# Feeding the first two token blocks of a fused layer partly from SBUF, squares taken from the sum, and the last gate moved to the activation

## The chip, the cores and the metric

The kernel runs on one core of a Trainium2 chip. Its engines are TensorE (PE in the profile; its weight loads are PEld), VectorE (DVE), ScalarE (ACT), GpSimd (POOL) and SyncE (SP), whose queue issues nearly all DMA transfers here. The metric is the device time of one execution in microseconds (us), as the median of several runs. A profile shows one execution; its span runs from the first to the last recorded instruction.

## What is computed

The reference is one layer with adaptive layer norm (batch 1, 2048 tokens, 448 channels, all float32):

```python
mod = (_silu(c) @ w_mod).reshape(c.shape[0], 6, 1, -1)
sa, ca, ga, sb, cb, gb = (mod[:, 0], mod[:, 1], mod[:, 2], mod[:, 3], mod[:, 4], mod[:, 5])
h = _layernorm(x, axis=-1) * (1 + ca) + sa
x = x + ga * _A_ref(h, ...)      # S4D convolution along the tokens, by FFT
h = _layernorm(x, axis=-1) * (1 + cb) + sb
x = x + gb * _B_ref(h, B_w1, B_b1, B_w2, B_b2)
```

`_A_ref` builds a kernel of length 2048 for each channel, convolves `h` with it by transforms of length 4096 and adds a skip term. `_B_ref` normalizes `h` once more, multiplies it along the token axis by `w1` (2048 to 1792), adds `b1`, applies the tanh form of GELU, multiplies by `w2` (1792 to 2048) and adds `b2`. The gate `gb`, one value for each channel, is `mod[5]` in the kernel.

## The kernel before

**Stages.** The first half of the time builds the convolution kernels and the spectrum of the input. Then comes the stage of the *pieces*. Piece n handles two of 32 frequency groups for one half of the channels (`DC` = 224 of 448): pieces 0 to 15 are the first half and run mixed with the stage before, pieces 16 to 31 the second half and run in the loop `for k in range(NP + 1)`. For each piece, `pc_load` fetches its spectrum `u` (3 buffers) and its tables `si` (4 buffers), `pc_tables` makes the missing table quarters on POOL, `pc_swap` makes a swapped copy of `u` on ACT, `pc_s2` transforms the kernel's part (`kx`, two PE products), `pc_mul` multiplies on DVE (`z`), `pc_inv` transforms back (`vv`, four PE products of 128x224), and `pc_out` copies the result from PSUM to a tile `vt` on ACT and writes it to `v_d` in HBM. `v_d` has 32 rows (frequency groups) of 128 by 448. In step k of the loop the kernel loads piece n + 3 (n = 16 + k), does `pc_s2` and `pc_mul` of n, the tables of n + 1, and `pc_inv` and `pc_out` of n - 1.

**Norm stage.** The last transform runs along the 32 frequency groups, so each of the 16 token blocks of 128 needs all 32 rows of `v_d`. For block r, `ln_load(r)` reads a tile `vt` of 128 partitions (32 groups by 4) and 2 times 448 columns back from `v_d`, and for odd r the next pair of `x` tiles (`x_pair`). `ln_y(r)` multiplies it by the table `ft` into PSUM (`y`, one buffer, two halves of 64 rows) and adds it to `x` on DVE with the sum taken along. `stats` then makes the mean (DVE), the sum of squares (ACT, `Square` with the mean as bias) and the root. `ln_mod(r)` applies the first norm and the modulation and takes the second statistics; `ln_out(r)` makes `h3`, split into a rounded part `h3h` and a rest `h3l`, so that each product becomes three products in the fast float format. `warm(n)` issues n dummy products.

**First product.** `mlp1` multiplies step r by seven tiles `acc` of PSUM, three products each, 21 in all. Weights come through `WeightStream`: load (SP), rounding (ACT), rest (DVE), four steps ahead. There are two halves of 16 steps with seven tiles each. Behind each, `gelu` reads the tiles: ACT makes `u` (3 buffers), DVE casts it to `uh` and subtracts for `ul`. PE goes on with the next half, whose tiles are the same PSUM banks.

**Second product.** For each of 16 token tiles, 42 products run into `o`; DVE then adds `b2`, multiplies by `mod[5]` and adds `x` read back from HBM, and the result is written out.

**Order.** PE, ACT, DVE and POOL execute in the order of the program text. SP's order is made by a scheduler up to the last four steps of the piece loop and written by hand from there, in two manual regions (`last` and `first`); a transfer without a dependence can still be lifted ahead of the second region. An instruction that waits holds up all behind it on its engine.

The lines that the prediction follows are L828 (`v_d<-vt`, the write of a piece), L1230 (the load of a block), L1250 (`y`), L1253 (adding `x`), L1240 and L1242 (mean and squares), L1222 to L1224 (`acc`), L1294 (`warm`), L1336 to L1338 (`gelu`), L1368 and L1369 (the end).

Of the kernel before, what the change touches and what calls it, by code (L numbers as in the profile page):

```python
# [22 lines left out]
P = 128  # L23
# [8 lines left out]
DC = 224  # L32
# [5 lines left out]
WAHEAD = 4  # L38


def dft_tables():
# [66 lines left out]
    order = lambda a: a.reshape(P, 32, 2, 2, 2, 16).swapaxes(3, 4)  # L108
# [11 lines left out]
    t["FT"] = ft.reshape(P, 64)  # L120

# [99 lines left out]
def tile_adaln_s4d_mixer(ctx, tc, i, out):  # L221
# [20 lines left out]
    with ExitStack() as es:  # L242
# [580 lines left out]
        def pc_out(n, copy=S.copy):  # L823
            c, p = divmod(n, NP)
            vt = swp.tile([P, 2, DC], F32, tag="vt", name="vt", bufs=4) if c else fp.tile([P, 2, DC], F32, tag="vt", name="vt")
            copy(vt, pv.pop(n))
            rows = v_d[2 * p : 2 * p + 2, :, c * DC : (c + 1) * DC]
# [342 lines left out]
        swp = es.enter_context(tc.tile_pool(name="swp", bufs=2))  # L1170
        pc_swap(NP)
        for k in range(NP + 1):
# [16 lines left out]

            if k == NP - 3:  # L1190
                wst.load()
                x_pair(0)

# [9 lines left out]
    with ExitStack() as es:  # L1203
# [9 lines left out]
        v_v = v_d.rearrange("k (ch g r) d -> r (k ch) g d", ch=4, g=2)  # L1213
# [12 lines left out]
        vts, hs, sa, sb = {}, {}, {}, {}  # L1226

        def ln_load(r):
            vts[r] = rot.tile([P, 2, D], F32, tag="vt", name="vt", bufs=4)
            nc.sync.dma_start(vts[r], v_v[r])  # L1230
            if r % 2 and 1 < r < 15:
                x_pair(r + 1)
# [4 lines left out]
        def stats(src, total, tag):  # L1237

            mean, ss, rs = (small(nm, tag) for nm in ("mean", "ss", "rs"))
            V.tensor_scalar(mean, total, -1.0 / D, None, ALU.mult)  # L1240
            sq = rot.tile([P, D], F32, tag="sq", name="sq")
            S.activation(sq, src, AF.Square, bias=mean, accum_out=ss)  # L1242
            S.activation(rs, ss, AF.Sqrt, scale=1.0 / D, bias=eps_t)
            return mean, rs

        def ln_y(r):
            y = py.tile([P, D], F32, tag="y", name="y")
            vt = vts.pop(r)
            for g in range(2):
                nc.tensor.matmul(y[64 * g : 64 * g + 64], ft, vt[:, g], start=True, stop=True)  # L1250
# [33 lines left out]
        for r in range(4):  # L1284
            ln_load(r)
            if r == 1:
                x_pair(2)
# [8 lines left out]
        for t in range(-3, 16):  # L1296
            if t < 0:
                warm((9, 1, 2)[t + 3])
# [33 lines left out]
        def gelu(acc, fh):  # L1332
            for f in range(7):
                k = 7 * fh + f
                u = ru.tile([P, D], F32, tag="u", name="u")
                S.activation(u, acc[f], AF.Gelu_apprx_tanh, bias=b1[:, k : k + 1])  # L1336
                V.tensor_copy(uh[fh][:, f], u)
                V.tensor_tensor(ul[fh][:, f], u, uh[fh][:, f].bitcast(F32), ALU.subtract)  # L1338
# [14 lines left out]
        for t in range(16):  # L1353
# [14 lines left out]
            V.scalar_tensor_tensor(y, o, b2[:, t : t + 1], mod[5], ALU.add, ALU.mult)  # L1368
# [29 lines left out]
```

## Time and profile before

| | |
|---|---|
| median of 3 runs | 698.07 us (697.39 to 699.43) |
| profiled execution | 699.5 us, its span 697.7 us |
| mean granted TensorE clock | 0.988 |
| PE busy | 646.5 us (93%) |
| DVE, ACT, POOL busy | 424.1, 448.5, 274.7 us |
| DMA moved | 128.04 MB, mean 184 GB/s |

A row of the timeline reads: start in us, duration in us, engine, line, operation, output<-inputs, the shape, how often, and in brackets how long the engine stood idle before it and what released it. Rows that follow each other closely are merged (x2, x4), and their duration is then that of the group; a float32 product shows as two records, so x2 is one such product. A row of the chain reads: start, duration, what. In the table by stretches a row has the stretch, its length, the busy time of PE, PEld, DVE, ACT and POOL with the count of instructions, the granted clock, the mean busy share of the 16 DMA engines, and GB/s. A group row has the line, engine, operation, count, busy us and mean ns of one, then the idle time before them.

### The profile page before, as it was taken

The numbers are of one execution on the slowest core, as the hardware profiler recorded it, in microseconds if no ns is written. First come the engines' busy times: TensorE is split into PE (matmuls) and PEld (weight loads), VectorE is DVE, ScalarE is ACT, GpSimd is POOL, SyncE is SP. The second block draws the span as 40 slices with busy tenths as digits, with TensorE's granted clock in tenths as the row PEclk, the third lists the DMA queues.
The fourth block names the chain that finished last, engine by engine and source line by source line (L and its number), as shares of the span: only waits on it lengthen the run. The fifth ranks groups of instructions, "written<-read, shape, count | busy, mean of one in ns | idle before, by whom it ended". The sixth has DMA issues, their size and how long they took to land.

```text
span 697.7 us, 18532 instructions
## 1 busy us (share of the span) xinstructions
PE 646.5 (93%) x7314; PEld 486.1 (70%) x7314; DVE 424.1 (61%) x811; ACT 448.5 (64%) x841; POOL 274.7 (39%) x364
## 2 busy tenths in 40 slices
PE   0868999999988899999999989999999999999997
PEld 0444454455545676676789747778999999999996
DVE  7877889787575584857744368777622354444431
ACT  5787698899879899999766568877422332222220
POOL 6694669588588767777546200000000000000000
PEclk9998999999999999999999999999999999999999
DMA  7595647588785486554579899974683445555640
GB/s 183 178 194 143 214 163 241 212 234 268 213 266 165 126 170 170 145 157 120 142 235 301 257 278 244 236 177 135 174 247 108 146 132 159 159 158 165 169 129 28
DMA packets 101894, 128.04 MB, mean 184 GB/s; under 512 B 13547, under 2 KB 85231, under 8 KB 101807
## 3 DMA queue, kind: packets, MB, share of 16 engines
q1 hardware_dynamic: 100606, 123.31, 63.0%
q0 software_dynamic: 1200, 3.54, 2.4%
q8 instruction: 58, 0.95, 0.6%
q14 instruction: 30, 0.24, 0.1%
HBM read 91.46 MB, written 34.87 MB: 181 GB/s over the span
## 4 chain that ended last, share of the span: by engine, by line
PE 68%; ACT 10%; DMA 8%; DVE 6%; issue 4%; POOL 3%; SPq 1%; DVEq 0%; ACTq 0%; POOLq 0%
PE xe L621 7%; PE acc L1222 7%; PE o L1365 6%; PE o L1364 6%; PE o L1366 6%; PE acc L1223 6%; PE acc L1224 6%; PE kg L711 6%; DMA si<-in_SK_dram 3%; PE xg L621 3%; PE pu L542 2%; PE pu L574 2%; PE vv L820 2%; PE kx L804 2%; PE vv L821 2%
## 5 line engine op out<-in xcount | busy, mean ns | idle before, releaser
L206 ACT CAST whi<-w 128x896 fp32r<-128x896 f32 x64 | 59.8, 938 | 134.9 <-PE o L1365 84.6
L215 DVE TENSOR_TENSOR wlo<-w,whi 128x896 fp32r<-128x896 f32 x64 | 68.1, 1088 | 43.1 <-ACT whi L206 36.8
L684 POOL TENSOR_TENSOR G<-mag,gs 128x512 f32<-128x512 f32 x56 | 71.9, 1283 | 50.9 <-ACT gs L680 47.1
L1222 PE MATMUL acc<-h3h,whi 128*128 128x448 f32 x224 | 82.7, 369 | 0.8 <-ACT h3h L1273 0.8
L1223 PE MATMUL acc<-h3l,whi 128*128 128x448 f32 x224 | 81.5, 364 | 0.7 <-DVE h3l L1280 0.5
L1365 PE MATMUL o<-ul,whi 128*128 128x448 f32 x224 | 81.3, 363 | 0.0
L1364 PE MATMUL o<-uh,whi 128*128 128x448 f32 x224 | 81.2, 362 | 0.0
L1224 PE MATMUL acc<-h3h,wlo 128*128 128x448 f32 x224 | 80.7, 360 | 0.0
L1366 PE MATMUL o<-uh,wlo 128*128 128x448 f32 x224 | 80.6, 360 | 0.0
L711 PEld LDWEIGHTS kg<-E,G 128*32 128x32 f32 x3584 | 56.6, 114 | 32.3 <-issue 22.2
L711 PE MATMUL kg<-E,G 128*32 128x64 f32 x3584 | 66.4, 228 | 6.7 <-issue 6.1
L685 POOL TENSOR_TENSOR G<-mag,gs 128x512 f32<-128x512 f32 x56 | 71.8, 1282 | 0.0
L621 PE MATMUL xg<-tab,lph 64*128 64x512 f32 x112 | 62.3, 556 | 5.1 <-ACT gs L680 2.4
L621 PE MATMUL xe<-tab,lph 64*128 64x512 f32 x112 | 62.2, 555 | 1.1 <-ACT gs L681 0.9
L686 DVE TENSOR_TENSOR E<-m,xe 128x512 f32<-128x512 f32 x53 | 36.4, 687 | 41.3 <-ACT xe L679 24.3
L1368 DVE SCALAR_TENSOR_TENSOR y<-o,b,mod 128x448 f32<-128x448 f32 x16 | 10.9, 684 | 80.2 <-PE o L1366 80.2
L665 POOL TENSOR_TENSOR m<-mag,w 128x512 f32<-128x512 f32 x53 | 56.0, 1056 | 4.3 <-DMA u<-us_d 0.2
L1222 PEld LDWEIGHTS acc<-h3h,whi 128*128 128x128 f32 x224 | 42.0, 188 | 13.9 <-ACT h L1278 5.6
L812 DVE TENSOR_TENSOR z<-kx,u 128x448 f32<-128x448 f32 x48 | 28.4, 620 | 27.7 <-PE kx L804 27.7
L1223 PEld LDWEIGHTS acc<-h3l,whi 128*128 128x128 f32 x224 | 42.1, 188 | 3.3 <-DVE h3l L1280 0.8
L1364 PEld LDWEIGHTS o<-uh,whi 128*128 128x128 f32 x224 | 42.0, 188 | 3.4
L621 PE MATMUL xe<-tab,lex 64*128 64x512 f32 x56 | 28.9, 531 | 16.6 <-DMA lex<-wm 15.8
(233 smaller groups left out, 1512.1 us busy)
## 6 DMA issues: line engine op xcount, KB each, us to landing
w<-in_B_w_dram SPq DMA_DIRECT2D x64, 224.0 KB
w<-in_B_w_dram SPq DMA_DIRECT2D x32, 448.0 KB
u<-us_d SPq DMA_DIRECT2D x48, 224.0 KB
yu_d<-yt SPq DMA_DIRECT2D x16, 448.0 KB
yi<-yu_d SPq DMA_DIRECT2D x32, 224.0 KB
us_d<-uo SPq DMA_DIRECT2D x16, 448.0 KB
v_d<-vt SPq DMA_DIRECT2D x32, 224.0 KB
vt<-v_d SPq DMA_DIRECT2D x16, 448.0 KB
```

Source lines behind the costliest of these rows:

```text
L206: self.nc.scalar.copy(hi, w)
L215: eng.tensor_tensor(lo, w, hi.bitcast(F32), ALU.subtract)
L621: T.matmul(out[k], lhs[r], rhs[r], start=start, stop=stop)
L684: G.tensor_tensor(Gt[:, 1], mg_, v32(sg), ALU.mult)
L685: G.tensor_tensor(Gt[:, 0], mg_, v32(cg_), ALU.mult)
L711: T.matmul(kg[32 * q : 32 * q + 32, m], Gt[:, c, d], E[:, c, d], start=h == 0 and c == 0 and m == 0, stop=h == 1 and c == 1, skip_group_ch ...
L1222: nc.tensor.matmul(acc[f], hi[:, fs], h3h[:, r], start=r == 0, stop=False)
L1223: nc.tensor.matmul(acc[f], hi[:, fs], h3l[:, r], start=False, stop=False)
L1224: nc.tensor.matmul(acc[f], lo[:, fs], h3h[:, r], start=False, stop=r == 15)
L1364: nc.tensor.matmul(o, hi[:, ks], uh[kh][:, k], start=kh == 0 and k == 0, stop=False)
L1365: nc.tensor.matmul(o, hi[:, ks], ul[kh][:, k], start=False, stop=False)
L1366: nc.tensor.matmul(o, lo[:, ks], uh[kh][:, k], start=False, stop=kh == 1 and k == 6)
```

## The change

1. **Blocks 0 and 1 don't wait for the last three pieces.** For these two blocks only 26 of the 32 rows of `v_d` are read for the second half of the channels (`v_load(r, 26)`, issued in step `NP - 2`); the last six rows of the first half of the channels come by four small loads in step 1. The missing products for the last three pieces are taken from their tiles `vt`, still in SBUF (`vlast`), times tables `fl` (masked so that each piece's rows meet only those of the block): six products of 128x128 by 224 columns for each block. `fl` is zeroed on POOL in three parts, and a quarter is loaded, in step 1.
2. **The rows of a token block lie together.** The order of the tables `I1` and `I2` is changed so that a block's 8 rows in each frequency group are contiguous in `v_d`; a load has 128 rows of 3584 bytes where it had 256 of 1792.
3. **Order.** The region `first` begins with `x_pair(2)` and then loads blocks 2 and 3. The nine dummy products before the first `y` go.
4. **Squares from the sum.** `Square` takes the sum as bias and -448 as scale, and the root 1/448^3; the mean is made beside it.
5. **Gate at the activation.** `u` is multiplied by `mod[5]` on DVE behind the GELU. In the second half the cast to `uh` moves from DVE to ACT, one tile behind. At the end `x` gets `mod[5] * b2` added, which needs no product, and one addition remains behind the last product.

```diff
+LAST = 3
...
-    order = lambda a: a.reshape(P, 32, 2, 2, 2, 16).swapaxes(3, 4)
+    order = lambda a: a.reshape(P, 32, 2, 2, 2, 16).transpose(0, 1, 5, 2, 4, 3)
...
+    fl = np.zeros((4, 4, 2, 2, 2 * LAST, 2, 64))
+    for r in range(2):
+        for g in range(2):
+            fl[r, :, g, r, :, g] = t["FT"].reshape(32, 4, 64)[-2 * LAST :].swapaxes(0, 1)
+    t["FL"] = fl.reshape(32, 2 * 2 * LAST * P)
...
+            if n >= 2 * NP - LAST:
+                vlast.append(vt)
...
+        v_v = v_d.rearrange("k (r ch g) d -> r k ch g d", ch=4, g=2)
+        end = 2 * (NP - LAST)
+        fl = swp.tile([P, 2, 2 * LAST, P], F32, name="fl", bufs=1)
+        vlast, vts = [], {}
+
+        def v_tile(r):
+            vts[r] = rot.tile([P, 2, D], F32, tag="vt", name="vt", bufs=4)
+
+        def v_load(r, k):
+            nc.sync.dma_start(vts[r][0 : 4 * k].rearrange("p g d -> p (g d)"), v_v[r, 0:k].rearrange("k ch g d -> k ch (g d)"))
...
+            if k == 1:
+                for q in range(1, 4):
+                    G.memset(fl[32 * q : 32 * q + 32], 0.0)
+                nc.sync.dma_start(fl[0:32].rearrange("p r q m -> p (r q m)"), i["FL"])
+                for r in range(2):
+                    v_tile(r)
+                    for g in range(2):
+                        nc.sync.dma_start(vts[r][4 * end :, g, 0:DC], v_v[r, end:, :, g, 0:DC])
             if k == NP - 3:
                 wst.load()
                 x_pair(0)
+            if k == NP - 2:
+                for r in range(2):
+                    v_load(r, end)
...
-        v_v = v_d.rearrange("k (ch g r) d -> r (k ch) g d", ch=4, g=2)
...
         def ln_load(r):
-            vts[r] = rot.tile([P, 2, D], F32, tag="vt", name="vt", bufs=4)
-            nc.sync.dma_start(vts[r], v_v[r])
+            v_tile(r)
+            v_load(r, 2 * NP)
...
-            V.tensor_scalar(mean, total, -1.0 / D, None, ALU.mult)
-            sq = rot.tile([P, D], F32, tag="sq", name="sq")
-            S.activation(sq, src, AF.Square, bias=mean, accum_out=ss)
-            S.activation(rs, ss, AF.Sqrt, scale=1.0 / D, bias=eps_t)
+            sq = rot.tile([P, D], F32, tag="sq", name="sq")
+            S.activation(sq, src, AF.Square, bias=total, scale=-float(D), accum_out=ss)
+            S.activation(rs, ss, AF.Sqrt, scale=1.0 / D**3, bias=eps_t)
+            V.tensor_scalar(mean, total, -1.0 / D, None, ALU.mult)
...
+            n = 4 * end
             for g in range(2):
-                nc.tensor.matmul(y[64 * g : 64 * g + 64], ft, vt[:, g], start=True, stop=True)
+                out = y[64 * g : 64 * g + 64]
+                if r > 1:
+                    nc.tensor.matmul(out, ft, vt[:, g], start=True, stop=True)
+                    continue
+                nc.tensor.matmul(out[:, 0:DC], ft, vt[:, g, 0:DC], start=True, stop=True)
+                nc.tensor.matmul(out[:, DC:], ft[0:n], vt[0:n, g, DC:], start=True, stop=False, skip_group_check=True)
+            for q in range(2 * LAST) if r < 2 else ():
+                p, k = divmod(q, 2)
+                nc.tensor.matmul(y[:, DC:], fl[:, r, q], vlast[p][:, k], start=False, stop=q == 2 * LAST - 1, skip_group_check=True)
...
-        for r in range(4):
+        x_pair(2)
+        for r in range(2, 4):
             ln_load(r)
-            if r == 1:
-                x_pair(2)
...
-                warm((9, 1, 2)[t + 3])
+                warm((0, 1, 2)[t + 3])
...
         def gelu(acc, fh):
+            us = {}
+
+            def split(f, copy):
+                copy(uh[fh][:, f], us[f])
+                V.tensor_tensor(ul[fh][:, f], us[f], uh[fh][:, f].bitcast(F32), ALU.subtract)
+
             for f in range(7):
                 k = 7 * fh + f
-                u = ru.tile([P, D], F32, tag="u", name="u")
-                S.activation(u, acc[f], AF.Gelu_apprx_tanh, bias=b1[:, k : k + 1])
-                V.tensor_copy(uh[fh][:, f], u)
-                V.tensor_tensor(ul[fh][:, f], u, uh[fh][:, f].bitcast(F32), ALU.subtract)
+                us[f] = ru.tile([P, D], F32, tag="u", name="u")
+                S.activation(us[f], acc[f], AF.Gelu_apprx_tanh, bias=b1[:, k : k + 1])
+                V.tensor_tensor(us[f], us[f], mod[5], ALU.mult)
+                if fh == 0:
+                    split(f, V.tensor_copy)
+                elif f:
+                    split(f - 1, S.copy)
+            if fh:
+                split(6, S.copy)
...
-            V.scalar_tensor_tensor(y, o, b2[:, t : t + 1], mod[5], ALU.add, ALU.mult)
-            V.tensor_tensor(y, y, xt, ALU.add)
+            V.scalar_tensor_tensor(xt, mod[5], b2[:, t : t + 1], xt, ALU.mult, ALU.add)
+            V.tensor_tensor(y, o, xt, ALU.add)
```

2 lines of the change are left out of this document (1 added, 1 removed).

## The prediction

> **What bounds the kernel now.** The page comes first: TensorE (PE) is busy 93% of the span, but the chain that ended last runs on it for 68% only. So the change is worth what it does at the places where PE is not the last.
>
> ```profile
> span 697.7 us, 18532 instructions
> PE 646.5 (93%) x7314; PEld 486.1 (70%) x7314; DVE 424.1 (61%) x811; ACT 448.5 (64%) x841; POOL 274.7 (39%) x364
> PE 68%; ACT 10%; DMA 8%; DVE 6%; issue 4%; POOL 3%; SPq 1%; DVEq 0%; ACTq 0%; POOLq 0%
> ```
>
> The table by stretches (PE, PEld, DVE, ACT, POOL busy, clock, DMA share, GB/s) shows two limits side by side in the stage of the pieces: PE without a gap and the DMA engines at 0.99. Just before, DMA has room (0.71). From 429 us on PE is full: what the norm stage starts earlier, it also ends earlier.
>
> ```profile
> 352.00:360.00 8.00, 7.38 (x95) 6.62 (x91) 3.82 (x7) 5.86 (x11) 4.13 (x7) 1.00 0.71 203
> 373.50:378.00 4.50, 4.50 (x26) 4.50 (x25) 2.31 (x4) 3.28 (x7) 3.38 (x8) 1.00 0.99 331
> 406.00:407.00 1.00, 0.33 (x2) 0.20 (x4) 0.61 (x3) 0.86 (x3) 0.00 (x0) 1.00 1.14 328
> 408.00:409.00 1.00, 0.47 (x1) 0.19 (x1) 0.67 (x2) 0.44 (x1) 0.00 (x0) 1.00 1.02 233
> 429.00:450.00 21.00, 21.00 (x101) 16.02 (x100) 15.98 (x49) 16.63 (x36) 0.00 (x0) 1.00 1.07 236
> ```
>
> Between these stages the chain and the timeline show the round trip that the change cuts: the last piece is copied to SBUF, written to HBM (3.22 us), its completion lets SyncE (SP) issue the load of block 0, and that lands at 401.37, 3.90 us later. Only then does the first `y` run.
>
> ```profile
> 393.61 0.54 ACT vt L826
> 394.17 3.22 DMA v_d<-vt
> 397.47 1.22 SPq L1230 DMA_DIRECT2D vt<-v_d  x2
> 401.37 0.97 PE L1250 MATMUL y<-vt,ft 128*64 128x448 f32 x4
> 402.39 0.62 DVE L1253 SCALAR_TENSOR_TENSOR xt<-xt,y 128x448 f32<-128x448 f32 x1 [0.92 <-DMA vt<-v_d]
> 406.67 0.97 PE L1250 MATMUL y<-vt,ft 128*64 128x448 f32 x4 [0.77 <-DVE xt L1253]
> 408.49 0.47 PE L1222 MATMUL acc<-h3h,whi 128*128 128x448 f32 x1 [0.85 <-ACT h3h L1273]
> 409.01 0.15 DVE L1240 TENSOR_SCALAR mean<-sum 128x1 f32<-128x1 f32 x1
> 409.19 0.67 ACT L1242 ACTIVATE sq<-xt,mean 128x448 f32<-128x448 f32 x1 [0.76 <-DVE mean L1240]
> 416.39 0.48 PE L1223 MATMUL acc<-h3l,whi 128*128 128x448 f32 x1 [0.54 <-DVE h3l L1280]
> ```
>
> **Start of the norm stage.** In the instruction order built from the changed kernel the two loads of 26 of 32 rows stand on SP behind the write of piece 29 and wait for piece 28's. That is the second of the two writes below: it issues at about 387.6 (its row ends at 387.98, one issue takes about 0.4) and, at 3.22 us like the last one, is done at 390.8. With 3.90 us for the load, block 0 is in SBUF at 394.8, behind the copy of the last piece (394.15). Call the delay that the piece stage picks up d: landing is 394.8 + d.
>
> ```profile
> 385.34 2.64 SPq L828 DMA_DIRECT2D v_d<-vt  x2
> 360.21 0.54 PE L820 MATMUL vv<-z,si 128*128 128x224 f32 x2
> 360.97 0.92 PE L804 MATMUL kx<-yk,si 128*128 128x224 f32 x4
> 402.27 1.02 PE L1294 MATMUL acc<-mod 128*128 128x448 f32 x2
> ```
>
> The first `y` gets longer. Six masked products at 0.38 us (360.21 to 360.97 holds two products of the same shape) are 2.3. The four half-width `ft` products are bounded by today's 0.97 (same columns in all) and 4 x 0.38 = 1.5; I take 1.2, as the two column halves now alternate in another order. So y(0) takes 3.5 and ends at 398.3 + d, against 401.37 + 0.97 = 402.34: 4.0 - d earlier.
>
> What is late next is y(1). It needs the PSUM tile back (0.62 + 0.08 + handover, 0.75), takes 3.5 instead of 0.97, and two warm-ups (0.76 each, the single one above with its drain 1.02) and y(2) (0.9) stand behind it on PE: 0.75 + 3.5 + 1.5 + 0.9 = 6.7 us from y(0)'s end to the first `acc` product, where today it is 408.49 - 402.34 = 6.15. That gives back 0.55. On the other side the squares start from the sum: `mean` (0.15 and a handover) leaves the chain four times, and block 1's squares, which stand idle 0.76 for a `mean` queued behind `h3l` on DVE, can start at once. So `h3l` of block 1, for which PE stalls until 416.39 (0.7 us behind its work), should be there first, and the stall goes. Net of both: +0.15, nothing. I keep 4.0 - d; on its own terms (landing +-0.8, `ft` +-0.3) 2.9 to 5.0 - d.
>
> The full loads of blocks 2 to 15 have half as many rows, each twice as long, and two blocks and one pair of `x` leave the crowded start; costed at nothing, since PE is full there.
>
> **Delay d of the piece stage.** The change adds 0.20 MB of table, 0.46 MB of `x` for blocks 2 and 3 (the new order lets the scheduler lift that pair ahead of piece 19's loads) and 0.09 MB in four small loads.
>
> ```profile
> 355.00 0.33 SPq L780 DMA_DIRECT2D si<-in_SK_dram  x1
> 359.69 0.37 SPq L828 DMA_DIRECT2D v_d<-vt  x1
> 360.31 0.32 SPq L772 DMA_DIRECT2D u<-us_d  x1
> 361.21 0.33 SPq L780 DMA_DIRECT2D si<-in_SK_dram  x1
> 363.48 4.03 DMA si<-in_SK_dram
> 389.29 1.24 SPq L1166 DMA_DIRECT2D xt<-in_A_u_dram  x2
> ```
>
> At 331 GB/s the 0.75 MB are 2.3 us of DMA; the free 0.29 of 352 to 360 is 2.3 us. So bytes alone cost between 0 and 2.3. SP is the sharper term: back-to-back issues take 0.62 each (1.24 for two), so the four small loads between the write at 359.69 and the `u` at 360.31 push piece 21's `si` from 361.21 to about 363.2. Its landing after 4.03 would be 367.2, where PE's pace of 2.27 per piece (four `vv` and two `kx` products at 0.38) wants it at 365.5: 1.7 late if the transfer is as slow as now, 0.5 if the emptied queue makes it a microsecond or so faster. Later pieces can't win it back, PE being full. I take d = 1.0, with 0 and 4.0 (SP and bytes in full) as ends.
>
> ```profile
> L315 POOL MEMSET lex<- 32x256 f32 x4 | 1.2, 340 | 0.0
> 355.14 0.84 POOL L797 TENSOR_SCALAR si<-si 64x256 f32<-64x256 f32 x1
> 357.91 0.39 POOL L795 COPY si<-si 64x256 f32<-64x256 f32 x1 [1.93 <-DMA si<-in_SK_dram]
> 363.99 0.54 PE L820 MATMUL vv<-z,si 128*128 128x224 f32 x2
> ```
>
> POOL gets three memsets of 1536 columns between the table copies of pieces 18 (end 355.98) and 19. By the 256-column row, in proportion, each is 6 x 0.34 = 2.0, together 6.1: until 362.1. Piece 19's copies take 1.8 and are wanted at 363.99: done at 363.9, hidden, by the wait for `si` that POOL has there anyway.
>
> **Activation.** DVE gets a third step for each of seven tiles.
>
> ```profile
> 488.08 2.49 ACT L1336 ACTIVATE u<-acc,b 128x448 f32<-128x448 f32 x4 [2.27 <-PE acc L1224]
> 488.75 0.39 DVE L1337 CAST uh<-u 128x448 fp32r<-128x448 f32 x1 [2.42 <-ACT u L1336]
> 489.18 0.63 DVE L1338 TENSOR_TENSOR ul<-u,uh 128x448 fp32r<-128x448 f32 x1
> 489.72 0.39 DVE L1337 CAST uh<-u 128x448 fp32r<-128x448 f32 x1
> 490.88 0.64 ACT L1336 ACTIVATE u<-acc,b 128x448 f32<-128x448 f32 x1 [0.32 <-DVE ul L1338]
> 495.50 3.09 DVE L215 TENSOR_TENSOR wlo<-w,whi 128x896 fp32r<-128x896 f32 x3
> 693.28 0.69 DVE y L1368
> 694.00 0.63 DVE y L1369
> ```
>
> Per tile DVE takes 0.97 now (488.75 to 489.72). The product with `mod[5]` has the shape of `ul` (0.63, with the handover 0.66), so 1.63 then. Three `u` buffers tie the activation of tile f to the `ul` of tile f - 3, as the row at 490.88 shows already: tile 3's is done at 488.75 + 1.63 x 3 + 0.66 + 0.43 + 0.62 = 495.35, and tile 6's activation ends near 496.1. PE makes a tile in three products of 0.2 (101 instructions in 21.0 us): the first accumulator is done at 488.05, six more tiles follow, and after six tiles of the next half, at 488.05 + 12 x 0.6 = 495.2, it wants the last accumulator. PE waits about 1.0; ends 0 and 2.0. Behind it on DVE the weight splits move by 7 x 0.66 = 4.6, from 495.50 to 500.1; the first is done 1.03 later at 501.1, and PE asks for it after two whole steps and two products, at 488.05 + 3.6 + 8.4 + 1.0 + 0.4 = 501.4: hidden, but at its edge.
>
> In the second half the cast goes to ACT. Each engine then has about 1.3 us per tile, the last tile is done some 10.5 us after the first accumulator, and PE asks for it after 3.6 + 4.2 (products on the first half) + 3.6 = 11.4: 0, with 1.0 as end.
>
> **Tail.** After the last product one DVE step is left: 694.00 - 693.28 = 0.72 gained, by the same `x` row's steps done before. The earlier 15 tiles are hidden under PE.
>
> **Sum.** -(4.0 - 1.0) + 1.0 - 0.7 = -2.7 us. The profiled execution took 699.5 (span 697.7, 1.8 around it), so it would take 696.8. It lies 1.4 above the median of the three runs (698.07; 697.39 to 699.43), so against that the forecast is 695.4. What a measurement of this kernel can tell from no change is about 0.3%, 2.1 us.
>
> **Rivals.**
> A: the piece stage pays SP and bytes in full, d = 1.7 + 2.3 = 4.0: -0 + 1.0 - 0.7 = +0.3, 698.4. For it: PE and DMA are both at their limit from 360 on. Against: the free DMA time just before.
> B (slower): POOL's memsets run at the pace of its arithmetic row, 0.84 for 256 columns, 15.1 us in all. Piece 19's copies end at 356.0 + 15.1 + 1.8 = 372.9, 8.9 late, and PE with them; d = 8.9 makes +5.2, 703.3. It decides slower from memsets of 12 us on. Against: the memset row itself.
> C: PE's clock. Nine warm-ups go, and PE is then empty from about 393.6 (the last piece's copy starts) to 394.8. In 406 to 409 PE was busy 0.33 and 0.47 of a microsecond and the granted clock stayed 1.00, so a gap of 1.3 us should not drop it. If it did, y(0) and y(1) would take 7 us more: +4.3, 702.4. The Trainium skill, "TensorE: Matmul & The Clock Gate", section "What's actually happening", says that the clock halves after an idle window of about 3.4 us; by that rule a gap of 1.3 us is safe as well, and C needs the gap to grow past it, through a late load.
> D: that the early load still waits for the last write is excluded by the built order.
>
> **Numbers.** Forecast case 0.55 (693.4 to 696.8; 0.47 of it faster by over 0.3%, 0.08 within), d at 0 and no wait at the activation 0.05 (693.0, faster), A 0.27 (0.24 within, 0.03 slower with an activation at its end of 2.0), B 0.08, C 0.05. That is faster 0.52, within 0.32, slower 0.16. The range 692.8 to 698.6 takes in the first three and leaves B, C and A's tail out, 0.16.
>
> **What would show it.** Right: y(0)'s `ft` products near 396, y(0) lasting about 3.5, the first `acc` product about 2.5 earlier, PE waiting about 1 us for the seventh activation, a single DVE step at the end. Wrong: piece 31's copy later than 395.5 (d), memset rows over 2 us, a granted clock under 1 after 395, or a PE gap in the second activation.

## The result and the profile after

The changed kernel takes 701.73 us (median of 12 runs, 700.63 to 704.94), beside 698.77 (12 runs, 697.15 to 702.83) for the kernel before on the same chip: a ratio of 1.0038, 95% interval 1.0022 to 1.0054. It is slower by about 0.4%, where 695.4 us was forecast and 698.6 was the upper end of the range. The profiled execution took 702.32 us with a span of 700.5, 2.8 us above the one before on both counts, so it can stand for the result.

The page:

```profile
span 700.5 us, 18568 instructions
PE 646.3 (92%) x7328; PEld 489.1 (70%) x7328; DVE 428.1 (61%) x818; ACT 452.4 (65%) x848; POOL 279.1 (40%) x367
PE 70%; ACT 12%; DVE 6%; DMA 5%; issue 4%; POOL 2%; SPq 1%; DVEq 0%; ACTq 0%; POOLq 0%
```

PE's busy time is the same, and DMA's part of the chain fell from 8% to 5%, as the change intends. The loss is visible only by place. The table by stretches shows it in the stretch that begins where the pieces end:

```profile
373.50:378.00 4.50, 4.26 (x23) 3.91 (x22) 1.76 (x4) 2.55 (x6) 2.46 (x6) 1.00 0.88 256
394.00:397.50 3.50, 0.34 (x2) 0.00 (x0) 0.24 (x2) 2.85 (x4) 0.00 (x0) 0.97 0.96 277
397.50:401.50 4.00, 2.25 (x10) 1.30 (x11) 0.92 (x1) 0.00 (x0) 0.00 (x0) 0.50 0.89 261
401.50:404.00 2.50, 2.50 (x8) 2.28 (x7) 0.00 (x0) 0.57 (x1) 0.00 (x0) 0.50 0.31 54
429.00:450.00 21.00, 21.00 (x101) 16.00 (x100) 16.06 (x48) 17.54 (x38) 0.00 (x0) 1.00 1.00 229
```

PE works 0.34 us of 3.5, and then at a granted clock of 0.50, while the DMA engines are busy at 0.9 and more. From 429 us on PE is full at full clock again. The timeline and the chain (its one row begins at 392.77 and says DMA) give the places:

```profile
353.76 1.68 PE L810 MATMUL kx<-yk,si 128*128 128x224 f32 x8
390.39 0.92 PE L810 MATMUL kx<-yk,si 128*128 128x224 f32 x4
394.42 0.53 ACT L832 COPY vt<-vv 128x448 f32<-128x448 f32 x1 [1.02 <-PE vv L827]
392.77 6.43 DMA vt<-v_d
399.25 1.02 PE L1284 MATMUL y<-vt,ft 128*64 128x224 f32 x4 [4.91 <-DMA vt<-v_d]
400.95 4.10 PE L1288 MATMUL y<-vt,fl 128*128 128x224 f32 x12
404.88 0.92 PE L1331 MATMUL acc<-mod 128*128 128x448 f32 x2
406.74 2.54 PE L1288 MATMUL y<-vt,fl 128*128 128x224 f32 x12
411.61 0.47 PE L1251 MATMUL acc<-h3h,whi 128*128 128x448 f32 x1
```

In the kernel before, two rows answer to the first two:

```profile
354.81 1.68 PE L804 MATMUL kx<-yk,si 128*128 128x224 f32 x8
389.48 1.02 PE L804 MATMUL kx<-yk,si 128*128 128x224 f32 x4 [0.20 <-DMA si<-in_SK_dram]
```

The first of each pair, two pieces back to back with 14 more behind them, is called the *head* below. Executions reach it up to 6 us apart whatever the kernel is (351.2 to 357.3 in the runs of this document); places are therefore told from the head on. The last `kx` stands 34.67 us behind it before and 36.63 after; the first `y` 46.56 (401.37) and 45.49; the first `acc` product 53.68 (408.49) and 57.85; the end of the span 342.9 and 346.7. So the early load brought `y` forward by 1.1 us, and by the first `acc` product 4.2 us were lost.

The rest of the change:

```profile
356.11 4.23 POOL L1211 MEMSET fl<- 32x1536 f32 x3
360.65 0.40 POOL L801 COPY si<-si 64x256 f32<-64x256 f32 x1 [0.32 <-DMA si<-in_SK_dram]
359.47 3.14 SPq L1216 DMA_DIRECT2D vt<-v_d  x4
366.04 1.02 PE L810 MATMUL kx<-yk,si 128*128 128x224 f32 x4 [0.69 <-DMA si<-in_SK_dram]
418.34 0.46 PE L1252 MATMUL acc<-h3l,whi 128*128 128x448 f32 x1
497.36 0.63 ACT L1379 ACTIVATE u<-acc,b 128x448 f32<-128x448 f32 x1 [0.98 <-DVE ul L1374]
498.05 0.47 PE L1251 MATMUL acc<-h3h,whi 128*128 128x448 f32 x1 [0.74 <-ACT u L1379]
696.37 0.62 DVE L1417 TENSOR_TENSOR y<-o,x 128x448 f32<-128x448 f32 x1 [7.19 <-PE o L1414]
697.02 0.33 SPq L1418 DMA_DIRECT2D out_dram<-y  x1
```

The memsets take 1.4 us each, and POOL then still waits for a DMA, so they are hidden. The four small loads hold SP for 3.14 us and `kx` waits for `si` behind them. The product with `h3l` of block 1 (418.34) has no wait in front any more. At the activation PE waits 0.74 us. The output is issued 0.65 us behind the start of the last DVE step (697.02 - 696.37), where it was 1.37 (694.65 - 693.28).

### The profile page after: what moved, and what is told of

Same layout as the page of the kernel before. It is cut to its first block, busy times and chain, and to the rows that moved or that the text cites. A ratio compares the mean times of both kernels' runs of the same rounds, so it can differ in the third digit from the quotient of the medians.

```text
span 700.5 us, 18568 instructions
## 1 busy us (share of the span) xinstructions
PE 646.3 (92%) x7328; PEld 489.1 (70%) x7328; DVE 428.1 (61%) x818; ACT 452.4 (65%) x848; POOL 279.1 (40%) x367
## 4 chain that ended last, share of the span: by engine, by line
PE 70%; ACT 12%; DVE 6%; DMA 5%; issue 4%; POOL 2%; SPq 1%; DVEq 0%; ACTq 0%; POOLq 0%
PE xe L627 7%; PE acc L1251 6%; PE o L1414 6%; PE o L1413 6%; PE o L1412 6%; PE acc L1252 6%; PE acc L1253 6%; PE kg L717 6%; PE xg L627 3%; PE pu L548 2%; PE kx L810 2%; PE pu L580 2%; DMA si<-in_SK_dram 2%; PE vv L826 2%; PE y L1282 2%
## 5 line engine op out<-in xcount | busy, mean ns | idle before, releaser
L717 PEld LDWEIGHTS kg<-E,G 128*32 128x32 f32 x3584 | 56.4, 114 | 31.0 <-issue 21.2
L692 DVE TENSOR_TENSOR E<-m,xe 128x512 f32<-128x512 f32 x53 | 36.3, 685 | 41.1 <-ACT xe L685 24.9
L1417 DVE TENSOR_TENSOR y<-o,x 128x448 f32<-128x448 f32 x16 | 10.0, 625 | 79.0 <-PE o L1414 79.0
L1413 PEld LDWEIGHTS o<-ul,whi 128*128 128x128 f32 x224 | 42.0, 188 | 3.4
```

Of the source, the lines that this page charges most:

```text
L717: T.matmul(kg[32 * q : 32 * q + 32, m], Gt[:, c, d], E[:, c, d], start=h == 0 and c == 0 and m == 0, stop=h == 1 and c == 1, skip_group_ch ...
L1413: nc.tensor.matmul(o, hi[:, ks], ul[kh][:, k], start=False, stop=False)
```

## The experiments

The first question was what the late `y` costs and why it is late. Theory: the early load waits in a DMA queue that is full; the gap takes PE's clock down. Rivals: the longer `y` themselves, or SP's four issues. All positions below are from the head, in us, and each row is one profiled execution: two kernels that are alike up to the early loads (the mended feed and its second version) have their last `kx` at 34.80 and 36.30.

| kernel | last `kx` | first `y` | first `acc` | span's end |
|---|---|---|---|---|
| before | 34.67 | 46.56 | 53.68 | 342.9 |
| after | 36.63 | 45.49 | 57.85 | 346.7 |
| six dummy products | 37.00 | 46.41 | 56.43 | 345.4 |
| weights behind | 36.70 | 44.26 | 58.17 | 348.9 |
| two small loads | 35.77 | 45.49 | 57.75 | 346.3 |
| early loads of other data | 39.18 | 42.97 (masked products) | 55.28 | 345.0 |
| block 0 alone early | 35.66 | 44.62 | 56.54 | 345.8 |
| weights and `x` at the head | 36.94 | 43.84 | 53.87 | 342.7 |
| feed, mended | 34.80 | 44.51 | 54.53 | 341.7 |
| no feed, items 2, 4, 5 | 34.54 | 47.00 | 53.74 | 341.6 |
| no feed, items 4, 5 | 34.70 | 47.50 | 54.24 | 342.1 |

**Clock: six dummy products in front of the first `y`.**

```diff
-                warm((0, 1, 2)[t + 3])
+                warm((6, 1, 2)[t + 3])
```

> The changed kernel with six dummy products ahead of the first y (it has none). Clock theory: in the changed kernel PE was empty for 4.9 us before the first y, the granted clock fell to 0.50 from 397.5 to 404, and y(0) lasted 5.8 us instead of 3.4. Six dummy products of 0.76 us fill 394.9 to 399.4; the clock stays at 1.00, y(0) lasts 3.4, the first acc product comes 2.4 us earlier (near 409.2), the time falls by about 2.4 us. Rival (the masked products are slow for a reason of their own, such as weights or waits): y(0) still lasts 5.8 and the time stays within 0.5 us of the changed kernel's.

Its table by stretches and its timeline:

```profile
397.50:401.50 4.00, 4.00 (x20) 2.38 (x19) 0.57 (x1) 0.00 (x0) 0.00 (x0) 1.00 0.73 221
399.36 0.60 PE L1284 MATMUL y<-vt,ft 128*64 128x224 f32 x4
400.28 2.54 PE L1288 MATMUL y<-vt,fl 128*128 128x224 f32 x12
```

The clock stays at 1.00 and y(0) lasts 3.3 us (399.36 to 402.65) instead of 5.6 (399.25 to 404.88). That the clock costs 2.3 us there is shown. The first `acc` gains only 1.4, since the six products end at 46.4, behind the landing. Time 702.07, ratio 1.0016 (0.9987 to 1.0045).

**Weights behind the early loads.**

```diff
-                wst.load()
                 x_pair(0)
...
                     v_load(r, end)
+                wst.load()
```

> The changed kernel with the first weight load (0.46 MB) issued behind the two early loads of blocks 0 and 1 instead of ahead of them. Queue theory: the early loads took 6.43 us because the weights, a pair of x and a piece's write (1.15 MB) stood ahead of them in the DMA queue at about 250 GB/s; without the weights they take about 4.6 us and issue up to 1 us earlier, block 0 lands 1.8 to 2.8 us earlier, and if the PE gap then stays short the clock stays up as well: time 1.8 to 4.5 us less. Rival (a load of 104 rows is slow by itself, or reads of rows just written are): 6.4 us from issue to use again, time unchanged within 0.5 us.

```profile
396.97 0.60 PE L1284 MATMUL y<-vt,ft 128*64 128x224 f32 x4 [3.62 <-DMA vt<-v_d]
410.88 0.47 PE L1251 MATMUL acc<-h3h,whi 128*128 128x448 f32 x1 [2.13 <-ACT h3h L1311]
```

With 0.46 MB less in front, `y` comes 1.2 us sooner, but the load still takes 6.1 us from its issue at 390.85, close to the rival's 6.4 and not the theory's 4.6. The rounding of the late weights stands ahead of block 0's squares on ACT, and PE waits 2.13 us there: 705.29, ratio 1.0074 (1.0043 to 1.0104).

**Two small loads instead of four.**

```diff
-                    for g in range(2):
-                        nc.sync.dma_start(vts[r][4 * end :, g, 0:DC], v_v[r, end:, :, g, 0:DC])
+                    nc.sync.dma_start(vts[r][4 * end :, :, 0:DC], v_v[r, end:, :, :, 0:DC])
```

> The changed kernel with the four small loads (24 rows of 896 bytes each) made as two of 24 x 2 rows: the same bytes, two issues less on SP. SP theory: the four issues held SP for 3.1 us and put piece 21's table load late; two take about 1.4, the last piece ends about 1.2 us earlier against the start of the stage, the time falls by about 1. Rival (the added 0.75 MB in a full DMA stage is the delay): the stage lasts as long as before the edit, time unchanged within 0.4 us.

The last `kx` comes 0.86 us sooner; `y` doesn't move, as it waits for the load in either case. Time 701.45, ratio 1.0001 (0.9959 to 1.0043), an interval that holds both kernels. In all runs with four small loads, but for the one that moves the early loads into the stage, the last `kx` is at 36.6 to 37.2; with two it is at 34.8 to 36.3. So SP's issues carry a part of the delay; executions 1.5 us apart don't say how much.

**Item 5 alone, on the kernel before.** The edits are those of the last two hunks of the diff.

> The kernel before with item 5 of the change alone (gate multiplied at the activation, one step at the end). By the prediction's steps: PE waits 1.0 us for the seventh activation of the first half, the end is 0.7 shorter, together +0.3: not to be told from before. Rival (weights behind the longer activation on DVE come late too, in either half): PE waits of 1 us and more in the steps behind it, +1 to +2 us.

700.24, ratio 0.9996 (0.9966 to 1.0026). PE waits 0.75 us at the activation, so what the end gains, the activation takes, as the sum had it.

**Early loads that bring other data.** The two loads fetch rows of `w1`, in step 2.

```diff
+            if k == 2:
+                for r in range(2):
+                    nc.sync.dma_start(vts[r][0 : 4 * end].rearrange("p g d -> p (g d)"), i["B_w1"][0 : 4 * end, 0 : 2 * D])
...
-            if k == NP - 2:
-                for r in range(2):
-                    v_load(r, end)
```

> The changed kernel, but the two early loads of 104 rows bring rows of the first weight matrix instead of rows of v_d and stand in step 2 of the piece loop, 13 steps earlier: blocks 0 and 1 are computed from other data, and nothing that y(0) reads comes through the crowded queue at the end. Theory (the early loads land late because of what is in the DMA queue, the gap takes the clock down, and behind them the last write and so the loads of blocks 2 and 3 are late too): PE goes from the last vv to y(0) with less than 1.5 us of idle time, the granted clock stays at 1.00, y(0) lasts 3.3 us, the last write is done about 3.5 us after its issue instead of 7.7, and the first acc product stands about 52 us behind the kx group at the head of the last pieces (57.9 in the changed kernel, 53.7 before). Time about 696.5. Rival (the loss lies in the two longer y and in the delay of the piece stage, the landing only fills time): first acc at 55 or more, time 700 or more.

```profile
366.20 1.02 PE L810 MATMUL kx<-yk,si 128*128 128x224 f32 x4 [2.01 <-DMA si<-in_SK_dram]
369.64 1.02 PE L1284 MATMUL y<-vt,ft 128*64 128x224 f32 x4
400.42 0.61 PE L1284 MATMUL y<-vt,ft 128*64 128x224 f32 x4 [1.65 <-DVE xt L1291]
401.75:405.15 3.40, 3.40 (x11) 3.08 (x10) 1.37 (x4) 1.88 (x4) 0.00 (x0) 0.50 0.96 342
```

The pieces are 2.55 us later than in the changed kernel (39.18), but that isn't the price of the 0.73 MB moved ahead. The waits of `kx` for `si` sum to 2.39 us, where they were 2.10 in the changed kernel. The rest is PE's own time: y(0)'s `ft` products, with nothing left to wait for, run among the pieces (369.64, so products too can be lifted ahead of their place in the text), and behind the wait of 2.01 us the clock is 0.50 from 367.6 to 371.0. The 42.97 of the table is the first masked product.

From the last piece PE goes on to y(0) without a gap, but y(1) waits for the add of y(0), which stands on DVE behind a weight split. After this gap of 1.65 us the clock is 0.50 for 3.4 us again. The first `acc` lies at 55.28, which is the rival's number (55 or more), though not by its mechanism alone: from the last `kx` to it 16.1 us pass, where it was 21.2 in the changed kernel and 19.0 before. With the landing free, the late pieces, the new wait and the two falls of the clock still lose 1.6 us to the kernel before. 700.12, ratio 1.0008 (0.9980 to 1.0035).

**Block 0 alone early.** Block 1 is loaded whole behind the last write.

```diff
-                for r in range(2):
-                    v_load(r, end)
+                v_load(0, end)
...
-                if r > 1:
+                if r > 0:
```

> The changed kernel with block 0 alone loaded early and completed from SBUF; block 1 is loaded whole behind the last write, as before. Theory (a queue of bytes at some 270 GB/s in front of the landing): 0.36 MB less, so y(0) starts about 1.3 us earlier against the kx group (44.2 us behind it instead of 45.5), the gap on PE is about 3.6 us, and the last write lands 1.3 earlier too. One long y less is 2.4 us of PE: first acc about 54.5 behind the kx group, time about 699. Rival (a load of 104 rows is slow by itself, whatever stands beside it): y(0) still 45.5 behind the kx group and time about 700.

```profile
394.08 0.90 SPq L1188 DMA_DIRECT2D vt<-v_d  x1
400.31 1.02 PE L1283 MATMUL y<-vt,ft 128*64 128x224 f32 x4 [5.01 <-DMA vt<-v_d]
```

Half the bytes of its own, and the load still takes 6.2 us: against a queue of bytes as the whole cause. `y` is earlier from the head only as the pieces are (35.66). 701.15, ratio 1.0023 (0.9990 to 1.0056).

**Each early load in two, of 64 and 40 rows.**

```diff
-                    v_load(r, end)
+                    v_load(r, 16)
+                    nc.sync.dma_start(vts[r][64 : 4 * end].rearrange("p g d -> p (g d)"), v_v[r, 16:end].rearrange("k ch g d -> k ch (g d)"))
```

> The changed kernel with each early load made as two, of 64 and of 40 rows. Same bytes, two more issues of 0.6 us on SyncE. Theory (queue of bytes): y(0) starts within 0.5 us of where it did, 45.5 us behind the kx group. Rival (104 rows in 26 groups of four spread over only some of the 16 DMA engines, and 64 rows use all of them): y(0) starts 1 us or more earlier.

```profile
394.28 0.54 SPq L1188 DMA_DIRECT2D vt<-v_d  x1
399.70 1.02 PE L1285 MATMUL y<-vt,ft 128*64 128x224 f32 x4 [3.60 <-DMA vt<-v_d]
```

5.4 us from the first issue to `y`, 1.1 less than whole, with one more issue in between. `y` starts 44.30 from the head, 1.2 sooner, as the rival had it. One execution, 703.07 us.

**Weights and `x` at the head of the piece loop.**

```diff
         pc_swap(NP)
+        wst.load()
+        x_pair(0)
...
             if k == NP - 3:
-                wst.load()
-                x_pair(0)
+                pass
```

> The changed kernel with the first weights and the first x pair (0.92 MB) loaded at the start of the piece loop instead of right in front of the two early loads. Theory (what stands in front in the DMA queue makes the early load late, and only there): 0.92 MB less in front at about 270 GB/s is 3.4 us, the load takes about 4 us from its issue, y(0) follows the last vv within 1.5 us and lasts 3.3 us. First acc about 53 us behind the kx group at the head of the last pieces (57.9 in the changed kernel), time about 697.5. Rival (the DMA engines are full through the whole piece stage, so bytes moved ahead only make the pieces late, as the 0.73 MB moved in the run with data from elsewhere did by 2.2 us): the last kx is 2 to 3.5 us later against the kx group, and first acc lands at 55 to 57.

```profile
392.00:395.00 3.00, 0.15 (x1) 0.00 (x1) 0.06 (x1) 2.74 (x4) 0.00 (x0) 1.00 0.91 262
395.00 0.60 PE L1285 MATMUL y<-vt,ft 128*64 128x224 f32 x4 [2.85 <-DMA vt<-v_d]
```

The load takes 5.2 us from its issue at 389.77, the gap is 2.85, and this time the clock holds. The first `acc` comes at 53.87, 4.0 us sooner than in the changed kernel and level with the kernel before. The pieces were 0.3 later, not 2 to 3.5: theory, though not with its 4 us. 700.24, ratio 1.0017 (0.9988 to 1.0046).

**Weights and `x` behind the early loads,** and the same with the loads in two.

```diff
-                wst.load()
-                x_pair(0)
+                pass
             if k == NP - 2:
                 for r in range(2):
                     v_load(r, end)
+                x_pair(0)
+                wst.load()
```

> The changed kernel with the first weights and the first x pair issued behind the two early loads instead of in front of them. Theory (bytes in front): only one write of a piece stands in front, so block 0 lands about 4 us after its issue instead of 6.5, and the gap of PE in front of y(0) is 2 to 2.5 us instead of 4.9; later the first add of x or the first weights are waited for, about 2 us. Rival (the load's own shape and latency): 6 us from the issue again.

> The same, with each early load made as two, of 64 and of 40 rows. If the shape is the cause, block 0 lands 1 us or more sooner after its first issue than in the run with whole loads; if bytes in front are, it lands at the same time within 0.5 us, or later by the 0.6 us of one more issue.

```profile
391.35 1.74 SPq L1188 DMA_DIRECT2D vt<-v_d  x2
396.94 0.61 PE L1285 MATMUL y<-vt,ft 128*64 128x224 f32 x4 [2.99 <-DMA vt<-v_d]
```

Here the DMA engines are almost idle in front (share 0.13 from 390 to the issue), and whole loads still take 5.6 us; in two they take 4.7 (391.19 to 395.92). So of the 2.6 us by which the load exceeded 3.90, about 0.9 were what stood in front and another 0.9 go by splitting (1.1 with the run above, 1.2 between the two mended feeds below). These are rough: four executions with the same things in front landed 6.2 to 7.3 us after their issue. One execution each, 701.41 and 700.50 us.

**104 or 128 rows from one and the same place.** The order of the last run, with rows of `w1` in place of `v_d`.

```diff
-                    v_load(r, end)
+                    nc.sync.dma_start(vts[r][0 : 104].rearrange("p g d -> p (g d)"), i["B_w1"][0 : 104, 0 : 2 * D])
```

> The run with the first weights and x pair behind the early loads, but the two early loads fetch 104 rows of 3584 bytes of the first weight matrix instead of v_d: blocks 0 and 1 are computed from other data. Shape theory (104 rows are issued and moved slower than 128): about 0.9 us of SyncE for each load and about 5.6 us from the first issue to the first use, as with v_d. Rival (what makes the load slow is reading v_d itself, just written, or the write in front): about 4 us.

> The same with 128 rows, a quarter more bytes. Shape theory: 0.55 to 0.6 us of SyncE for each load, and 3.9 us or less from the first issue to the first use, over 1 us less than with 104 rows. Rival (shape counts for nothing): the same time as with 104 rows or up to 0.5 us more, for the bytes.

The chain of 104 rows, then of 128:

```profile
390.43 6.36 DMA vt<-in_B_w_dram
```

```profile
395.98 5.19 DMA vt<-in_B_w_dram
```

By one execution of each, 128 rows land 1.2 us sooner with a quarter more bytes, so the shape counts, and that the data lie in `v_d` is not what makes the load slow. Both numbers are above what was expected, and why is not shown: `x` follows 1.0 us behind the first load, but it did so within 1.3 us in the kernel before, where 128 rows took 3.90. SP's time for an issue did not follow the shape (about 0.4 us each with either, beside 0.8 to 0.9 with `v_d`). The Trainium skill, "DMA: Bandwidth & Descriptors", section "Why a DMA increments its semaphore by 16 and not by 1", says that a transfer uses the largest number of engines up to 16 that divides the slowest dimension on both sides: that would be 13 for 26 groups or 104 rows and 16 for 128. The trace agrees, by the semaphore updates that it keeps: each load of 104 rows has 13 that come 3.5 us or more after its issue (and one within 1.4), each of 128 rows has 16, and the parts of 64 and 40 rows have 16 and 10. By that rule every engine has 8 rows to move, with 104 as with 128, so the count of engines alone does not make the 1.2 us. About half of it is one late engine: all the others were done at 4.22 of the 6.36 us and at 3.71 of the 5.19.

**Item 5 with seven `u` buffers,** on the kernel before.

```diff
-                us[f] = ru.tile([P, D], F32, tag="u", name="u")
+                us[f] = ru.tile([P, D], F32, tag="u", name="u", bufs=7)
```

> The kernel before with item 5 alone (gate at the activation), and seven u buffers instead of three. Theory (the 1.0 us lost at the first activation comes from the three u buffers, and 0.7 us are won at the end): no wait of PE at the first activation, DVE later by 4.6 us with the weight splits still in time, time 0.7 us below the kernel before, ratio 0.999. Rival (DVE's extra 4.6 us meet the weight splits): a wait of PE for wlo of about 1 us two steps into the second half, ratio 1.000.

```profile
498.25 0.47 PE L1224 MATMUL acc<-h3h,wlo 128*128 128x448 f32 x1 [0.81 <-DVE wlo L215]
```

The rival was right: the wait at the activation went, and the split of the weights, which the prediction had found hidden at its edge, is now late by 0.8 us. 700.73, ratio 1.0005 (0.9977 to 1.0032).

**Without the feed.** Items 2 and 4 on the kernel before, and item 5 mended: seven `u` buffers, gate products first, then casts on ACT and subtractions on DVE.

```diff
             for f in range(7):
...
                 S.activation(us[f], acc[f], AF.Gelu_apprx_tanh, bias=b1[:, k : k + 1])
                 V.tensor_tensor(us[f], us[f], mod[5], ALU.mult)
+            for f in range(7):
+                S.copy(uh[fh][:, f], us[f])
+                V.tensor_tensor(ul[fh][:, f], us[f], uh[fh][:, f].bitcast(F32), ALU.subtract)
```

> The kernel before with items 2 and 4 (rows of a block together, squares from the sum) and a mended item 5: seven u buffers, the gate's product behind each activation, then all casts on ACT and all subtractions on DVE. Blocks 0 and 1 are loaded whole, and the nine dummy products stay. Theory (the loss comes from item 1, the rest is worth what the prediction said): no wait at the first activation and none for wlo after it, 0.7 us less at the end, 0.7 us less in front of block 1's h3l, so about 1.4 us below the kernel before, ratio 0.998. Rival (the longer rows or the squares cost something that the early loads cover in the changed kernel): ratio 1.000 or more, with a wait at the loads of blocks 0 to 3.

```profile
488.16 4.23 ACT L1337 ACTIVATE u<-acc,b 128x448 f32<-128x448 f32 x7 [2.29 <-PE acc L1224]
488.83 4.22 DVE L1338 TENSOR_TENSOR u<-u,mod 128x448 f32<-128x448 f32 x7 [2.44 <-ACT u L1337]
496.72 3.09 DVE L215 TENSOR_TENSOR wlo<-w,whi 128x896 fp32r<-128x896 f32 x3
```

The seven activations run without a stop, DVE begins the splits 7.9 us after its first gate product (488.83 to 496.72) instead of 11.4 (490.69 to 502.05), and PE has no wait from there to the end. 697.52, ratio 0.9963 (0.9937 to 0.9989): the one version whose interval lies below the kernel before, and in its trace 1.3 us shorter from the head on, about half of that 0.4%. The same **without item 2**:

> The run without the feed, and without item 2 as well: the kernel before with squares from the sum and the mended gate at the activation. If the 0.4% come from items 4 and 5 (2 x 0.7 us in the traces), the ratio is 0.997 to 0.998; if the longer rows carry a part, it is 0.999 or more, and the loads of blocks 0 to 3 land later.

699.33, ratio 1.0003 (0.9974 to 1.0031). Its trace lies 0.5 us behind the last one from the head on, 47.50 to the first `y`. That the longer rows make this is not shown: among runs with the short rows alone `y` starts between 46.56 and 47.54. The times differ by more, and their intervals overlap. How the 0.4% divide among items 2, 4 and 5, and how much of it is real, is not settled.

**Without the feed, weights and `x` at the head.**

> The run without the feed, with the first weights and the first x pair loaded at the start of the piece loop. Theory (a queue at the last write and the first load): write and load of the last piece take 1 to 2 us less than 7.8 in all, first acc 1 to 2 us earlier against the kx group than 53.7, ratio about 0.996. Rival (DMA engines full through the stage): the last kx later by 2 to 3 us, and the first acc too, ratio about 1.001.

```profile
361.21 1.86 PE L804 MATMUL kx<-yk,si 128*128 128x224 f32 x4 [2.55 <-DMA si<-in_SK_dram]
```

The rival's numbers came: last `kx` at 39.18, first `acc` at 57.5, 701.23, ratio 1.0018 (0.9990 to 1.0046). In the same place the loads cost the piece stage 0.3 us with the feed and 4.6 without. In both, PE waits once for `si` there, 2.71 us with the feed, where it stands in place of the 2.10 us of such waits that the changed kernel has, and 2.55 without. Behind the second wait the clock was 0.50 from 361.25 to 364.66, and PE, busy all that time, lost 1.7 us; behind the first it stayed at 1.00. So the DMA engines are not all of the 4.6 us.

**The feed, mended:** six dummy products, two small loads, the mended item 5; then with four dummy products and the loads in two.

> The changed kernel with three repairs: six dummy products in front of the first y (clock), the four small loads made two (SyncE), and item 5 mended as in the run without the feed. Theory: y(0) 2.5 us shorter, the pieces 0.9 us earlier, and 1.0 us less at the activation, 4 us less than the changed kernel if all of it counts, about 698 and ratio 0.999; the y landing 45.5 us behind the kx group bounds it, so 699 if the pieces' 0.9 us only lengthen the wait. Rival (the feed costs more than that by itself): ratio 1.002 or more.

```profile
397.22 0.61 PE L1283 MATMUL y<-vt,ft 128*64 128x224 f32 x4 [0.31 <-DMA vt<-v_d]
407.24 0.47 PE L1250 MATMUL acc<-h3h,whi 128*128 128x448 f32 x1
```

> The changed kernel repaired as before (two small loads, mended item 5), with four dummy products and each early load made as two of 64 and 40 rows. If the split load lands 1 us sooner, y(0) follows the dummy products at about 43.5 us behind the kx group at the head of the last pieces (44.5 in the repaired run), first acc at 53.5, ratio about 0.997; if not, PE waits about 1.5 us behind the dummy products and the ratio is 0.9985 as in the repaired run.

698.21, ratio 0.9985 (0.9959 to 1.0010), and 698.60, ratio 0.9997 (0.9971 to 1.0023), the second with `y` at 44.38 and the first `acc` at 55.10. Its pieces ended 1.5 us later; from the last `kx` to `y` it took 8.1 us instead of 9.7, as the split load promised, but PE then waited 0.63 us for `h3h`. The 0.85 us of the mended run's first `acc` against the kernel before (54.53 to 53.68) is the feed itself: `y` starts 2.05 us sooner, and from there to the first `acc` it takes 10.0 us (397.22 to 407.24) instead of 7.1.

## Why the prediction was wrong

By its own steps, from the head on (head of the kernel before at 354.81):

| step | predicted | measured | off by |
|---|---|---|---|
| delay d of the pieces | 1.0 | 1.96 | +0.96 |
| issue of the early load | 394.8 + d less 3.90, so 37.09 | 39.01 | +0.96 beyond d |
| load of block 0, to the first `y` | 3.90 | 6.48 | +2.58 |
| start of y(0) | 40.99 | 45.49 | +4.50, the three above |
| y(0) | 3.5 | 5.63 | +2.13 |
| end of y(0) to first `acc` | 6.7 | 6.73 | 0 |

The steps sum to 51.19 for the first `acc` and it came at 57.85: 6.7 us, of which the execution's 1.05 us shorter way to the head hides one. Forecast -2.7, measured +2.8.

- **The step that failed is the landing: "With 3.90 us for the load".** That row was of a load of 128 partitions, issued when the DMA share had fallen: 0.80 until it landed. The early load has 104 rows and stands behind 1.15 MB (weights, `x`, a write) in a stage whose DMA share the prediction itself quoted as 0.99; it took 6.48 at a share of 0.98. The runs show, roughly, 0.9 us for what stands in front and 0.9 to 1.2 for the whole load of 104 rows; half a microsecond or more of the 2.6 stays unassigned. The bound was wrong too: no end of the range let the load take more than 3.90 + 0.8.
- **d was mis-sized.** 1.96 instead of 1.0, inside its ends of 0 and 4.0. SP's hold was foreseen (3.14 us of issues), its price put too low; with half the issues d was 0.1 to 1.6 in four executions.
- **The rest of the late issue** has two parts. The write of piece 28 went out at 389.08, 35.32 from the head, where 387.6 + 1.0 makes 33.79: 0.57 more than d at the last `kx` says. And the load followed 3.69 us behind that write, not 3.30, because SP was issuing all the while, a term that the sum did not have:

```profile
389.08 0.37 SPq L836 DMA_DIRECT2D v_d<-vt  x1
389.50 1.25 SPq L192 DMA_DIRECT2D w<-in_B_w_dram  x2
390.79 1.24 SPq L1174 DMA_DIRECT2D xt<-in_A_u_dram  x2
392.13 0.53 SPq L836 DMA_DIRECT2D v_d<-vt  x1
392.77 1.78 SPq L1188 DMA_DIRECT2D vt<-v_d  x2
```

The write itself had landed at 391.46 by its last semaphore update, 2.38 us after its issue and less than the 3.22 assumed: it held nothing up.

- **Rival C came about,** a late load and then half the clock. Its 702.4 us is within 0.7 of the median, but by other parts: it charged 7 us to the clock on both `y`, where y(0) alone was hit by 2.1 to 2.3 and y(1) took 3.3 at 1.00, and nothing to the late load itself, 4.5. Its chance of 0.05 was wrong with the landing, as it rested on a gap of 1.3 us.
- **Right:** six masked products at full clock in 2.4 to 2.5 us and y(0) in 3.3 (3.5 said); y(0)'s end to the first `acc` 6.7; the stall for block 1's `h3l` gone; POOL's memsets hidden, at 4.2 us in all instead of 6.1; PE's wait at the activation 0.74 us (1.0 said, for want of `u` buffers, as the run with seven showed); no wait in the second half; the end 0.72 shorter. The final write took 0.4 longer, which no step had.
- **Not seen:** with the loads in front, the last write's completion slipped. The first loads behind it went out 7.1 us after its issue (395.23 to 402.32, blocks 2 and 3), where it was 3.3 (394.17 to 397.47, blocks 0 and 1). PE was late anyway, so it cost nothing here, but it bounds the gain: in the run with weights and `x` behind the split loads, y(2) waited 2.28 us for block 2.

## What to carry to other kernels

A load's duration may be taken from a row only if the row has its shape and the same things in front of it; in a stretch where the DMA share is near 1, starting a transfer earlier moves it behind the others and makes them late. Look at the granted clock in the stage that a transfer is moved into: in two runs here a part of what looked like its price was a fall of the clock. Dummy products that fill a wait look useless until the wait grows; before taking them away, price the work behind them at half the clock. When a change bundles several parts, time the bundle without its largest one: here the small parts, one of them mended, came out 0.4% faster (interval 0.1 to 0.6%) where the bundle lost 0.4%.

## What the runs showed of the hardware that was not expected

The clock's fall depends on where a gap of PE lies, not on its length alone. From 340 us to the end of PE's work, gaps of 1.65, 2.01, 2.13, 2.28, 2.55, 2.70 and 2.99 us and all from 3.60 us up were followed by a clock of 0.50; gaps of 2.19, 2.71 and 2.85 us and all of 1.39 us and less were not. So 2.7 us stands on both sides (128 rows of `w1`, and weights and `x` at the head).

The traces show what decides. Each of these falls lasts 3.41 or 6.83 us, and all falls of an execution begin at whole multiples of 3.413 us from each other: in the changed kernel the one at 397.31 comes 47 such steps behind the one at 236.89. Cut into these steps, PE was idle for 1.86 to 3.41 us of the step just before twelve of the thirteen falls, and for 1.65 us before the other (the second fall of the run with other data). In the steps at full clock with no fall behind them it was idle for 1.68 us at most: the gaps of 2.71 and 2.85 us are cut by a step's end into 1.68 + 1.03 and 1.20 + 1.65. So the limit lies at about half a step (1.65 to 1.86 us of 3.41), and a gap is safe or not by how it falls on the steps. This holds for the stages here; around 190 to 220 us, with other products, the changed kernel has a step with 1.96 us of idle time and no fall behind it, and one with 1.12 and a fall.

The Trainium skill, "TensorE: Matmul & The Clock Gate", section "What's actually happening", describes a free-running window of 3413 ns, and the traces agree. But the gaps of 1.65 to 2.99 us are under the idle window of about 3.4 us that the section names, so a gap need not fill a window: the measurement decides. The prediction's gap of 1.3 us, which it called safe by rows with gaps of 0.77 and 0.85, would have passed by all runs; the late load made it 4.91.
